# First tiles centred by a broadcast column of sums, first products by halves, the last block by rows

## The chip, the cores and the metric

The kernel runs on one core of a Trainium2 chip. The metric is the device time of one execution in microseconds (us). Engines are named as in the profile: PE is TensorE (matmuls), PEld its weight loads, DVE is VectorE, ACT is ScalarE, POOL is GpSimd, SP is SyncE; SPq, ACTq and POOLq are the places where these issue DMAs. "L694" is line 694 of the kernel before.

## What is computed

Linear attention with a norm, then a two-layer block with layer norm and a residual. There are 8 batches, 8 heads, 576 tokens and 64 features per head, so x has 512 features; the hidden layer has 2048.

```python
kv  = einsum('bhsd,bhse->bhde', k, v)              # 64 x 64 per head
o   = einsum('bhsd,bhde->bhse', q, kv)
x   = o / sqrt(mean(o*o, -1) + 1e-6) * g_norm      # then heads side by side: 512 features
xn  = (x - mean(x)) / sqrt(var(x) + 1e-6) * g_ln
out = x + relu(xn @ w1) @ w2
```

Inputs and output are float32; products run in bf16 and accumulate in float32. The factor 1/sqrt(var) isn't applied to xn: relu lets it pass, so it is multiplied in at the end (`rstd`).

## The kernel before

**Tiles and blocks.** A tile is 128 tokens. Each batch gives four tiles (512 tokens), which are one block; the 64 tokens that are left over in each of the 8 batches form a ninth block, "rem". A tile's path is: `o` (four PE products with kv), `sq` (ACT square), `red` (DVE sum per head), `root` (ACT), reciprocal, `y` and `x` (DVE, scaling), centring (`xc`), and the turn of the centred tile to features by tokens (`xT_blk`), by PE or by DMA. Block b's `mm1(b, ...)` (L684) multiplies `xT_blk` with w1 in groups of one PSUM bank: 16 matmuls with 128 tokens each (one tile at a time, L694), or 4 with 512. ACT applies relu behind each group (L697) and writes m1. `mm2` multiplies m1 with w2.

**mm2 in seven products.** For blocks 1 to 7 and rem, m1 and w2 are seen as 2 x 2 blocks and multiplied with seven products instead of eight (`mm2_seven`, L547, and for rem `mm2_seven_last`, L621). Sums of blocks of m1 (S1 to S4, L515 to L518) come from DVE, sums of blocks of w2 (T1 to T4) were made once. A product is eight matmuls for each of two tiles (`product`, L521, matmuls at L527). p_x and p_y are each made of two products that add up in one bank; of p_y, DVE reads the first product's result (L566) before the second is added.

**Order.** The order of each engine's queue is the order of the program text, written out by hand. `at(slot, fn)` (L769) files a piece of work under a slot of an agenda, and `tick()` (L778), which is called ahead of each group of matmuls, runs what is due. A slot is 1/32 of a block's time; the second half of a block with seven products has 14 ticks, so there slots are pressed together by 14/16. `plan_tile(s, ...)` (L455) files a tile's first part (`o`, `sq`, `red`) at s, its second (reciprocal, `y`, `x`, `xc_w`) at s + 2, and its turn. With at_o = 115 the fourth tile of batch 4 has its first part in tick 110 and its second in tick 112. These lie in batch 3's `mm2`: tick 110 stands ahead of p_q's first tile, 111 ahead of its second; 112 and 113 ahead of p_y's (S2 with T2). S4 (L517) and S3 (L518) are filed at 110 and 111, ahead of anything else in that tick. `var` of another tile (L419, ACT) stands at tick 113, slot 118.1.

**The start.** While the inputs land, the first two tiles of batch 0 go a short way (`x_b`, L318): one DVE instruction makes xb = og / rms in bf16 and sums its rows into `st`. `mean_b` (L326) makes a 128 x 128 diagonal matrix of these sums, for tile 0 on ACT (L330), for tile 1 on DVE (L332). `turn_b` (L334) turns xb by four PE products with the identity and adds to each a product of `mean_sb` (all -1/512, stationary) with that diagonal (moving), which subtracts the mean (L344). Features 0 to 255 are in one bank, 256 to 511 in another. ACT scales the first half with g_ln in two instructions (L355), DVE the second half in one (L357); g_ln by feature, `g_lnT_sb`, comes from a small PE product `glT` (L852) and a DVE copy (L858). `turn_first` and `turn_groups` (L209, L198) turn q of batch 0 by 64 x 64 PE transposes, 16 for each tile. `fill` (L214) puts idle products on PE.

In tick 1, between the first group of `mm1` for tile 0 and that for tile 1, stands `before_1` (L866): the transposes of q for tiles 2 and 3, then `t[1].turn_b()`, then `t[2].o()` and what follows on it. Groups of `mm1` use pool `ps1` with three banks; `t[1].o_g` holds one of them until `t[1].x_g` in tick 2.

**The end.** `mm2_seven_last` (L621) goes through rem's two tiles of each row half one after the other (`for t in range(2)`): for t the products p_x (first), p_q, p_y (first), p_z, p_y (second), store of the second row half (`put(1)`), p_x (second), S4 with b22, store of the first row half (`put(0)`). A `put` issues two DMAs of 64 partitions, one from SP, one from `upper`, ACT or SP. The last S4 product is made in two halves of 128 columns, and the last store in two of 256.

## Time and profile before

| what | value |
|---|---|
| median of 3 runs | 278.20 us (278.18 to 278.21) |
| the profiled execution | 278.19 us |
| its span, first to last instruction | 276.0 us |
| granted PE clock, mean | 0.998 |
| busy PE, DVE, ACT, POOL | 268.8, 197.7, 185.5, 116.6 us |
| first product of `mm1` (L694) | at 14.75 us |
| `mm1` of block 0 to the first product of `mm2` (L716) | 14.75 to 32.43 us |
| `mm2` of batch 3 | 121.7 to 135.8 us |
| `mm2` of rem, its last product | 259.4 to 271.8 us |
| last DVE add | ends at 272.17 us |

The span runs from the first to the last instruction of the program; some 2.2 us of the execution lie outside it. The timeline gives, for each instruction or run of like ones: start, length, engine, line, operation, output<-inputs, shapes, count and, in brackets, how long the engine stood idle before and which event ended that. Matmuls are pipelined: one of 128 columns is recorded with 0.22 us, while they start every 0.056 us. So the length of a run of them is their number times the pace and a drain. The chain is followed back from the last instruction, at each step to what released it.

### The profile page before, as it was taken

The numbers are of one execution on the slowest core, as the hardware profiler recorded it, in microseconds if no ns is written. First come the engines' busy times: TensorE is split into PE (matmuls) and PEld (weight loads), VectorE is DVE, ScalarE is ACT, GpSimd is POOL, SyncE is SP. The second block draws the span as 40 slices with busy tenths as digits, with TensorE's granted clock in tenths as the row PEclk, the third lists the DMA queues.
The fourth block names the chain that finished last, engine by engine and source line by source line (L and its number), as shares of the span: only waits on it lengthen the run. The fifth ranks groups of instructions, "written<-read, shape, count | busy, mean of one in ns | idle before, by whom it ended". The sixth has DMA issues, their size and how long they took to land.

```text
span 276.0 us, 6784 instructions
## 1 busy us (share of the span) xinstructions
PE 268.8 (97%) x2674; PEld 194.8 (71%) x2674; DVE 197.7 (72%) x464; ACT 185.5 (67%) x414; POOL 116.6 (42%) x143
## 2 busy tenths in 40 slices
PE   8899999999999999999999999999999999999993
PEld 3589855999889986468745874587458745874683
DVE  6676437897996895999679856985797379823564
ACT  3567755898759685768576857786877487746610
POOL 8842440991099007901870196017101800280140
PEclk9999999999999999999999999999999999999999
DMA  7999999979979993996299829960711161005032
GB/s 215 199 207 205 197 194 192 202 179 194 113 123 158 184 187 83 151 221 125 31 190 252 116 34 189 246 118 19 171 21 20 21 171 21 20 19 154 1 76 78
DMA packets 63880, 36.57 MB, mean 132 GB/s; under 512 B 34016, under 2 KB 60900, under 8 KB 63848
## 3 DMA queue, kind: packets, MB, share of 16 engines
q0 software_dynamic: 29104, 19.34, 47.9%
q1 hardware_dynamic: 34152, 15.81, 27.8%
q10 hardware_dynamic: 592, 0.98, 1.0%
q8 instruction: 21, 0.34, 0.5%
q14 instruction: 11, 0.09, 0.1%
HBM read 36.71 MB, written 9.44 MB: 167 GB/s over the span
## 4 chain that ended last, share of the span: by engine, by line
PE 84%; DVE 7%; DMA 4%; ACT 2%; issue 1%; POOL 1%; DVEq 0%; POOLq 0%
PE p L694 41%; PE p_y L527 8%; PE p_z L527 8%; PE p_x L527 8%; PE p L716 5%; PE p_s L527 4%; DMA w_sb<-in_moe_w_ch_dram 4%; PE p_q L527 4%; PE o_ps L302 2%; PE kv_ps L275 2%; DVE ss L379 1%; DVE S L517 1%; ACT m L697 1%; DVE o_ps L383 1%; DVE x_blk L401 1%
## 5 line engine op out<-in xcount | busy, mean ns | idle before, releaser
L694 PE MATMUL p<-xT_blk,w_sb 128*128 128x128 bf16 (+2 forms) x1024 | 131.7, 286 | 0.6 <-DMA w_sb<-in_moe_w_ch_dram 0.3
L694 PEld LDWEIGHTS <-w_sb 128*128 128x128 bf16 x1024 | 78.7, 98 | 44.9 <-issue 0.7
L697 ACT ACTIVATE m<-p 128x512 bf16<-128x512 f32 x144 | 85.5, 598 | 35.2 <-PE p L694 33.0
L527 PEld LDWEIGHTS <-m 128*128 128x128 bf16 x512 | 49.4, 98 | 7.7 <-issue 0.6
L379 DVE TENSOR_REDUCE ss<-sq 128x8 f32<-128x512 f32 x35 | 23.8, 680 | 24.6 <-ACT sq L308 24.4
L527 PEld LDWEIGHTS <-S 128*128 128x128 bf16 x392 | 37.5, 98 | 4.5 <-DVE S L516 0.3
L582 POOL TENSOR_TENSOR q<-q,x_blk 128x512 f32<-128x512 f32 x5 | 6.4, 1290 | 69.7 <-ACT q L561 69.7
L527 PE MATMUL p_x<-w_sb,m 128*128 128x256 bf16 x224 | 27.3, 273 | 0.0
L419 ACT ACTIVATE dev<-x_blk,st_blk 128x512 f32<-128x512 f32 x36 | 26.0, 722 | 0.3 <-DVE st_blk L405 0.2
L609 POOL TENSOR_TENSOR u<-u,x_blk 128x512 f32<-128x512 f32 x7 | 8.9, 1268 | 39.5 <-DVE u L566 39.5
L383 DVE TENSOR_TENSOR o_ps<-o_ps,inv 128x512 f32<-128x512 f32 x33 | 23.1, 700 | 3.1
L401 DVE SCALAR_TENSOR_TENSOR x_blk<-o_ps,g_norm_sb 128x512 f32<-128x512 f32 x33 | 22.8, 691 | 1.1
L308 ACT ACTIVATE sq<-o_ps 128x512 f32<-128x512 f32 x35 | 21.0, 599 | 3.6 <-PE o_ps L302 3.6
L515 DVE TENSOR_TENSOR S<-m 128x768 bf16<-128x768 bf16 (+2 forms) x22 | 12.7, 582 | 12.2 <-ACT m L697 12.2
L426 DVE TENSOR_SCALAR xc<-x_blk,st_blk 128x512 bf16<-128x512 f32 x32 | 18.6, 581 | 1.1
L387 ACT ACTIVATE rms<-ss,eps_sb 128x8 f32<-128x8 f32 x36 | 10.8, 299 | 11.7 <-DVE ss L379 11.3
L566 DVE SCALAR_TENSOR_TENSOR u<-p_y,rstd,v 128x256 f32<-128x256 f32 x28 | 12.2, 476 | 5.3 <-PE p_y L527 5.3
L716 PE MATMUL p<-w_sb,m 128*128 128x512 bf16 x64 | 15.0, 379 | 0.0
L561 ACT ACTIVATE v<-p_x,rstd 128x256 f32<-128x256 f32 x28 | 11.0, 478 | 5.3 <-PE p_x L527 5.3
L527 PE MATMUL p_y<-T,m 128*128 128x256 bf16 x112 | 13.9, 272 | 0.2 <-DVE u L566 0.2
L527 PE MATMUL p_z<-w_sb,S 128*128 128x256 bf16 x112 | 13.5, 273 | 0.0
L527 PE MATMUL p_y<-T,S 128*128 128x256 bf16 x112 | 13.5, 273 | 0.0
(149 smaller groups left out, 367.6 us busy)
## 6 DMA issues: line engine op xcount, KB each, us to landing
out_dram<-o_sb SPq DMA_DIRECT2D x26, 256.0 KB, 4.5
w_sb<-in_moe_w_ch_dram POOLq DMA_DIRECT2D x6, 512.0 KB, 13.7
q_in<-in_q_dram POOLq DMA_DIRECT2D x7, 320.0 KB, 6.5
k_in<-in_k_dram POOLq DMA_DIRECT2D x7, 320.0 KB, 7.7
v_in<-in_v_dram POOLq DMA_DIRECT2D x7, 320.0 KB, 9.9
q_in<-in_q_dram POOLq DMA_DIRECT2D x8, 256.0 KB, 7.2
k_in<-in_k_dram POOLq DMA_DIRECT2D x7, 256.0 KB, 8.4
v_in<-in_v_dram POOLq DMA_DIRECT2D x7, 256.0 KB, 12.3
```

What stands on the lines that cost most here:

```text
L308: nc.scalar.activation(self.sq_t, self.o_ps, func=AF.Square)
L379: nc.vector.tensor_reduce(self.ss, self.sq_t, axis=AX.X, op=ALU.add)
L383: nc.vector.tensor_mul(self.o_ps, self.o_ps, self.inv().to_broadcast([128, H, D]))
L401: nc.vector.scalar_tensor_tensor(x_blk[:, ts].rearrange("p (h d) -> p h d", h=H), in0=self.o_ps, scalar=1.0, in1=g_norm_sb.to_broadcast([1 ...
L419: nc.scalar.activation(dev, x_blk[:, ts], func=AF.Square, bias=st[:, 1, ts:ts + 1], accum_out=st[:, 2, ts:ts + 1])
L426: nc.vector.tensor_scalar_add(self.xc_t, x_blk[:, self.ts], st[:, 1, self.ts:self.ts + 1])
L515: for i, fn in enumerate((lambda: nc.vector.tensor_add(S1, a21, a22), lambda: nc.vector.tensor_sub(S2, S1, a11), lambda: nc.vector.tensor_ ...
L527: nc.tensor.matmul(dst[:, t - ts[0], :c1 - c0], lhsT=a[:, i, t * 128:(t + 1) * 128], rhs=w[:, i, c0:c1], start=start and t == ts[0] and i ...
L566: V.scalar_tensor_tensor(dst[:, t], in0=src[:, t], scalar=rstd[:, 2 * rows + t:2 * rows + t + 1], in1=other[:, t], op0=ALU.mult, op1=ALU.add)
L694: nc.tensor.matmul(p1[:, i, :], lhsT=w1_sb[:, kk, de * 128:(de + 1) * 128], rhs=blk[2][:, kk, sl], start=(kk == 0), stop=(kk == nK - 1))
L697: nc.scalar.activation(m1[:, de0:de0 + per, sl], p1, func=AF.Relu)
L716: nc.tensor.matmul(p2[:, c0:c1], lhsT=m1s[b][:, de, ts * 128:(ts + 1) * 128], rhs=w2_sb[:, de, c0:c1], start=(de == 0), stop=(de == nDe - 1))
```

## The change

Six edits:

- `mean_b` makes no diagonal: it copies the tile's sums (one column, 128 x 1) into bf16 `total_sb` on DVE. The centring product has this column, broadcast to 128 columns with step 0, as its stationary operand and `mean_sb` as the moving one; `mean_sb` is now the identity times -1/512, made on DVE behind `four_sb`, and no longer set by a memset at the start.
- `glT` and its copy move up, ahead of `turn_first(1)`.
- `t[0].turn_b()` is written ahead of `t[1].root()`, and in `before_1` `t[1].turn_b()` stands between the transposes for tile 2 and those for tile 3.
- `mm1`: the first group of tiles 0 and 1 goes through features 0 to 255 of all four hidden blocks, then 256 to 511. In all groups only the first matmul has the start flag and only the last the stop flag.
- `mm2_seven_last` becomes a generator with two parts for each tile, taken in the order first part of tile 0, of tile 1, second part of tile 0, of tile 1. Tile 0's `put(1)` now issues both DMAs from SP, and its `put(0)` the upper one from ACT. PSUM banks are taken accordingly.
- The fourth tile of batch 4 is filed at 116.2 instead of 115: first part in tick 111, second in 113, behind the `var` of slot 118.1.

```diff
@@ -129,10 +129,10 @@
     fill_sb = consts.tile([128, 512], bf16)
     gate = consts.tile([1, 1], bf16)
     mean_sb = consts.tile([128, 128], bf16)
+    total_sb = consts.tile([128, 2], bf16)
     gl_rows = consts.tile([nK, 128], f32)
     four_sb = consts.tile([nK, nK], f32)
     g_lnT_sb = consts.tile([128, nK], f32)
-    nc.vector.memset(mean_sb, -1.0 / Dm)
     nc.vector.memset(fill_sb, 0.0)
     nc.sync.dma_start(k_f[:, :HP // 2], pairs(k, 0, HP // 2))
     nc.scalar.dma_start(k_f[:, HP // 2:], pairs(k, HP // 2, HP))
@@ -323,13 +323,10 @@
                 self.xb, in0=self.og_ps, scalar=1.0, in1=self.i, op0=ALU.mult, op1=ALU.mult,
                 accum_out=st[:, 0, self.ts:self.ts + 1])
 
-        def mean_b(self, on_act=False):
-            self.diag = work.tile([128, 128], bf16, tag="diag", name="diag")
-            total = self.blk[1][:, 0, self.ts:self.ts + 1]
-            if on_act:
-                nc.scalar.activation(self.diag, identity, func=AF.Copy, scale=total)
-            else:
-                nc.vector.tensor_scalar_mul(self.diag, identity, total)
+        def mean_b(self):
+
+            ts = self.ts
+            nc.vector.tensor_copy(total_sb[:, ts:ts + 1], self.blk[1][:, 0, ts:ts + 1])
 
         def turn_b(self):
             ts = self.ts
@@ -341,7 +338,7 @@
                                  rhs=identity, start=True, stop=False)
 
             def centred(kk):
-                nc.tensor.matmul(tps[kk // 2][:, kk % 2], lhsT=mean_sb, rhs=self.diag,
+                nc.tensor.matmul(tps[kk // 2][:, kk % 2], lhsT=total_sb[:, ts:ts + 1].to_broadcast([128, 128]), rhs=mean_sb,
                                  start=False, stop=True)
 
             turned(0)
@@ -357,7 +354,7 @@
             nc.vector.tensor_mul(dst[:, 2:], tps[1],
                                  g_lnT_sb[:, 2:].rearrange("p (k o) -> p k o", o=1)
                                  .to_broadcast([128, 2, 128]))
-            del self.xb, self.diag
+            del self.xb
 
 
         def x_g(self, mean=False):
@@ -625,32 +622,34 @@
         b11, b21, b22 = w2_q(0, 0), w2_q(1, 0), w2_q(1, 1)
         x_all, _, o_sb = outs(b)
         v0_t, v1_t, qv_t, w22_t, u2_t = (half(fpool, n, n) for n in ("v0", "v1", "u3", "r5", "u2"))
-        banks = (((ps1, "p1"), (ps1, "p1"), (ps2, "p2"), (ps2, "p2"), (ps_m, "misc")),
-                 ((ps1, "p1"), (ps1, "p1"), (ps_out, "ops"), (ps_out, "ops"), (ps1, "p1"),
-                  (ps2, "p2")))
-        for t in range(2):
+        banks = (((ps1, "p1"), (ps1, "p1"), (ps2, "p2"), (ps2, "p2")),
+                 ((ps1, "p1"), (ps_out, "ops"), (ps_out, "ops"), (ps2, "p2")))
+        ends = (((ps_m, "misc", 0, C2),),
+                ((ps1, "p1", 0, C2 // 2), (ps2, "p2", C2 // 2, C2)))
+
+        def scaled_add(dst, src, r, other):
+            V.scalar_tensor_tensor(dst, in0=src, scalar=r, in1=other, op0=ALU.mult, op1=ALU.add)
+
+        def tile_of(t):
+
             def x(rows, cols):
                 return x_all(rows, cols)[:, t]
 
             def o(rows, cols):
                 return o_sb[rows][:, t, cols * C2:cols * C2 + C2]
 
+            def bank(pool, tag):
+                return pool.tile([128, 1, C2], f32, tag=tag, name="p_s")
+
             def part(dst, a, w, start, stop, c0=0, c1=C2):
                 product(dst, a, w, start, stop, (t,), c0, c1)
 
             def put(rows, c0=0, c1=Dm, upper=nc.scalar):
                 store(b, 2 * rows + t, o_sb[rows][:, t:t + 1], c0, c1, upper)
 
-            ends = ((0, C2),) if t == 0 else ((0, C2 // 2), (C2 // 2, C2))
-            p_x, p_q, p_y, p_z, *p_l = (pool.tile([128, 1, C2], f32, tag=tag, name="p_s")
-                                        for pool, tag in banks[t])
+            p_x, p_q, p_y, p_z = (bank(*e) for e in banks[t])
             v0, v1, qv, w22, u2 = (a[:, t] for a in (v0_t, v1_t, qv_t, w22_t, u2_t))
             r0, r1 = (rstds[b][:, 2 * rows + t:2 * rows + t + 1] for rows in range(2))
-
-            def scaled_add(dst, src, r, other):
-                V.scalar_tensor_tensor(dst, in0=src, scalar=r, in1=other,
-                                       op0=ALU.mult, op1=ALU.add)
-
             part(p_x, a11, b11, True, False)
             nc.scalar.activation(v1, p_x[:, 0], func=AF.Copy, scale=r1)
             nc.scalar.activation(v0, p_x[:, 0], func=AF.Copy, scale=r0)
@@ -667,19 +666,28 @@
             part(p_y, S3, T3, False, True)
             scaled_add(o(1, 0), p_y[:, 0], r1, qv)
             scaled_add(o(1, 1), p_y[:, 0], r1, w22)
-            put(1)
+            put(1, upper=nc.scalar if t else nc.sync)
+            del p_q, p_y, p_z
+            yield
             part(p_x, a12, b21, False, True)
             scaled_add(o(0, 0), p_x[:, 0], r0, x(0, 0))
             if t:
                 put(0, 0, C2)
-            for p, (c0, c1) in zip(p_l, ends):
+            for pool, tag, c0, c1 in ends[t]:
+                p = bank(pool, tag)
                 part(p, S4, b22, True, True, c0, c1)
                 scaled_add(o(0, 1)[:, c0:c1], p[:, 0, :c1 - c0], r0, u2[:, c0:c1])
+                del p
+            del p_x
             if t:
                 put(0, C2)
             else:
-                put(0, upper=nc.sync)
-            del p, p_l, p_x, p_q, p_y, p_z
+                put(0)
+            yield
+
+        tiles = [tile_of(0), tile_of(1)]
+        for t in (0, 1, 0, 1):
+            next(tiles[t])
 
     def mm1(b, t0, n, c0=0, c1=nDe):
         blk, m1 = blks[b], m1_of(b)
@@ -688,12 +696,16 @@
         for de0 in range(c0, c1, per):
             tick()
             p1 = ps1.tile([128, per, n * 128], f32, tag="p1", name="p1")
-            for i in range(per):
+
+            order = ([(i, kk) for k0 in (0, 2) for i in range(per) for kk in (k0, k0 + 1)]
+                     if b == 0 and t0 < 2 and de0 == 0 else
+                     [(i, kk) for i in range(per) for kk in range(nK)])
+            for i, kk in order:
                 de = de0 + i
-                for kk in range(nK):
-                    nc.tensor.matmul(p1[:, i, :], lhsT=w1_sb[:, kk, de * 128:(de + 1) * 128],
-                                     rhs=blk[2][:, kk, sl],
-                                     start=(kk == 0), stop=(kk == nK - 1))
+
+                nc.tensor.matmul(p1[:, i, :], lhsT=w1_sb[:, kk, de * 128:(de + 1) * 128],
+                                 rhs=blk[2][:, kk, sl], start=(i, kk) == order[0],
+                                 stop=(i, kk) == order[-1], skip_group_check=True)
             nc.scalar.activation(m1[:, de0:de0 + per, sl], p1, func=AF.Relu)
             del p1
             if b in (1, 2) and t0 + n == 4 and de0 + per in SPLIT_2:
@@ -788,6 +800,7 @@
     nc.vector.stream_shuffle(g_ln_sb, gl_row, [0] * 32)
     del gl_row
     nc.vector.tensor_copy(four_sb, identity[:nK, :nK])
+    nc.vector.tensor_scalar_mul(mean_sb, identity, -1.0 / Dm)
 
     qts[0] = qt_pool.tile([128, JJ, HP, 128], bf16, tag="qt", name="qt")
     held[0] = kv_pack[0]
@@ -839,6 +852,10 @@
     kv_b.times_g()
     part_red(kv_a)
     part_red(kv_b)
+    glT = ps1.tile([128, nK], f32, tag="p1", name="glT")
+    nc.tensor.matmul(glT, lhsT=gl_rows, rhs=four_sb, start=True, stop=True)
+    nc.vector.tensor_copy(g_lnT_sb, glT)
+    del glT
     turn_first(1, ps_m, "misc")
     t[0].root()
     t[0].o_g(ps2, "p2")
@@ -848,26 +865,22 @@
     turn_first(J, ps_m, "misc")
     t[1].o_g(ps1, "p1")
     fill(1, dead)
-    glT = ps1.tile([128, nK], f32, tag="p1", name="glT")
-    nc.tensor.matmul(glT, lhsT=gl_rows, rhs=four_sb, start=True, stop=True)
     fill(1, dead)
     del dead
     t[0].x_b()
-    t[0].mean_b(True)
+    t[0].mean_b()
     t[1].red()
-    nc.vector.tensor_copy(g_lnT_sb, glT)
-    del glT
+    t[0].turn_b()
     t[1].root()
-    t[0].turn_b()
     t[1].x_b()
     t[1].mean_b()
 
 
     def before_1():
         turn_first(2, ps_m, "misc", nc.vector.tensor_copy)
+        t[1].turn_b()
         tp = ps2.tile([128, HP, 128], bf16, tag="p2", name="tp")
         turn_groups(tp, 3, 0, H)
-        t[1].turn_b()
         t[2].o()
         t[2].sq()
         nc.scalar.copy(qts[0][:, 3], tp)
@@ -962,7 +975,7 @@
     at(268, lambda: rstd_of("rem"))
 
 
-    for b, at_q, at_o in ((3, 52, (68.5, 72.5, 76.5, 83)), (4, 81, (96.5, 102.7, 109, 115)),
+    for b, at_q, at_o in ((3, 52, (68.5, 72.5, 76.5, 83)), (4, 81, (96.5, 102.7, 109, 116.2)),
                           *((b, 32 * b - (46.4 if b == 5 else 47.2), tuple(32 * b - i for i in (34.5, 27.3, 20.1, 12.9)))
                             for b in range(5, B))):
         at(at_q, lambda b=b: turn_q_dma(b))
```

## The prediction

> **What bounds the kernel.** I read the page first (busy time, chain by engine, groups), then the chain in order of time, then the timeline of each engine where the change puts its hand.
>
> ```profile
> PE 268.8 (97%) x2674; PEld 194.8 (71%) x2674; DVE 197.7 (72%) x464; ACT 185.5 (67%) x414; POOL 116.6 (42%) x143
> PE 84%; DVE 7%; DMA 4%; ACT 2%; issue 1%; POOL 1%; DVEq 0%; POOLq 0%
> ...
> L694 PEld LDWEIGHTS <-w_sb 128*128 128x128 bf16 x1024 | 78.7, 98 | 44.9 <-issue 0.7
> ```
>
> TensorE is busy for 97% of the span, so an edit can win only where TensorE waits, or ahead of its first and behind its last product. The change removes no product. It touches three places: the first two tiles (about 13 to 20 us), the second half of batch 3 (121 to 136) and the last block (from 259). A busy share hides stalls there, because a matmul's recorded duration overlaps the next one's; so I measure groups of 16 products by their length.
>
> The profiled execution took 278.19 us, the median is 278.20; 2.2 us lie outside the span and stay.
>
> **First tiles.** Timeline rows of PE, ACT, DVE and POOL, then one row of the chain for the steady pace:
>
> ```profile
> 14.75 1.20 PE L694 MATMUL p<-xT_blk,w_sb 128*128 128x128 bf16 x16 [0.35 <-DMA w_sb<-in_moe_w_ch_dram]
> 15.73 0.22 PE L694 MATMUL p<-xT_blk,w_sb 128*128 128x128 bf16 x1
> 15.88 0.31 PE L204 MATMUL tp<-identity,q_in 64*64 64x64 bf16 x8
> 16.50 0.29 PE L340 MATMUL tp<-identity,xb 128*128 128x128 bf16 x2
> 17.41 1.26 PE L694 MATMUL p<-xT_blk,w_sb 128*128 128x128 bf16 x16
> 18.73 1.06 PE L694 MATMUL p<-xT_blk,w_sb 128*128 128x128 bf16 x16
> 13.14 0.29 PEld L852 LDWEIGHTS glT<-four_sb,gl_rows 4*128 4x128 f32 x2 [0.26 <-issue]
> ...
> 13.45 0.40 ACT L330 ACTIVATE diag<-identity,st_blk 128x128 bf16<-128x128 bf16 x1
> 14.27 0.63 ACT L355 ACTIVATE xT_blk<-tp,g_lnT_sb 128x128 bf16<-128x128 f32 x2
> 16.99 0.63 ACT L355 ACTIVATE xT_blk<-tp,g_lnT_sb 128x128 bf16<-128x128 f32 x2 [0.36 <-PE tp L344]
> 17.51 0.60 ACT L308 ACTIVATE sq<-o_ps 128x512 f32<-128x512 f32 x1
> 18.87 0.30 ACT L387 ACTIVATE rms<-ss,eps_sb 128x8 f32<-128x8 f32 x1 [0.29 <-DVE ss L379]
> 19.08 0.58 ACT L697 ACTIVATE m<-p 128x512 bf16<-128x512 f32 x1
> ...
> 9.31 0.35 DVE L259 CAST kv_pack<-even 64x192 bf16<-64x192 f32 x1 [0.96 <-PE odd L254]
> 13.87 0.15 DVE L858 COPY g_lnT_sb<-glT 128x4 f32<-128x4 f32 x1
> 15.01 0.69 DVE L322 SCALAR_TENSOR_TENSOR xb<-og_ps,inv 128x512 bf16<-128x512 f32 x1
> 15.74 0.54 DVE L332 TENSOR_SCALAR diag<-identity,st_blk 128x128 bf16<-128x128 bf16 x1
> 18.16 0.68 DVE L379 TENSOR_REDUCE ss<-sq 128x8 f32<-128x512 f32 x1
> ...
> 14.98 0.69 POOL L98 DMA_DIRECT2D q_in<-in_q_dram  x1 [1.66 <-DMA w_sb<-in_moe_w_ch_dram]
> 20.67 0.68 POOL L97 DMA_DIRECT2D v_in<-in_v_dram  x1 [1.87 <-DMA w_sb<-in_moe_w_ch_dram]
> ...
> 48.63 0.89 PE p L694 x16
> ```
>
> An undisturbed group takes 1.06 with its drain (18.73). The first two take 1.20 and 1.26: 0.14 and 0.20 lost inside them, waiting for the second half of the turned x.
>
> Tile 0: the 0.40 ACT diagonal goes, and a one-column DVE copy comes (0.15, from L858, the nearest small copy). It starts as soon as x's sum is read out, so the centring products no longer wait for the diagonal that ends at 13.85, and both halves of x are ready about 0.2 earlier. The first product itself doesn't move: it waits for w_sb's landing. Gain: the 0.14 inside the group. By halves, the wait for features 256 to 511 is covered by eight products of 0.056. The glT products (0.29 of loads, some 0.3 in all) only change places with the fill products ahead of the same turn: nothing. They now stand ahead of turn_first(1) and delay its ACT copy and tile 0's root by some 0.05, absorbed because TensorE, not xb, sets that turn. The new mean_sb multiply falls into a DVE wait of 0.96 for the kv products (at most L332's 0.54): nothing.
>
> Tile 1: its root now stands behind tile 0's two L355, so it comes at about 14.57, 0.6 later. DVE's reciprocal stood behind tile 0's multiply until 14.78 anyway; xb ends near 15.83 instead of 15.70, and the column copy at 16.02 instead of the diagonal at 16.28. With half of the 32 small transposes behind it, the turn starts near 16.10 instead of 16.50, L355 at 16.58 instead of 16.99, and the second group ends near 18.29 instead of 18.67: 0.36 to 0.38 ahead at this point.
>
> Most of that is not kept. Behind the turn stands t[2].o(), which now comes no earlier: TensorE goes from full to quarter tiles and back once more (15.73 to 15.88 where the pace is 0.056: 0.10 per switch). Its square (17.51) moves to about 17.42 only, because ACT was its releaser before and the products are now. The chain square, reduction (18.16), root (18.87), then L697 of the second group (19.08, ends 19.66) moves with it by 0.09. The fourth group needs the second's accumulators: the pool has three, and one holds tile 1's og until its x is written. TensorE would reach the fourth group at 18.73 + 0.89 = 19.62, ahead of 19.66; so this end decides already now. **Kept: 0.09.** Above: the third piece of w_sb (POOL's wait for it ends at 20.67; for the first piece POOL resumed at 14.98, 0.23 behind TensorE) lets the fifth group start at about 20.43, 0.15 ahead of the 20.6 that the groups' pace gives now. Below: a broadcast stationary operand has no row. The nearest are LDWEIGHTS of 98 ns and glT's two of 0.15 each; at the latter, four extra loads of 0.05 plus two switches of 0.10 give up to 0.2 lost, through sq of tile 2. I take 98 ns, the same type and width. Range: -0.15 to +0.2.
>
> By the Trainium skill (TensorEngine Tiling (Array Packing), Key Properties) a change of tiling mode drains TensorE. It speaks against turning the second tile between the two groups of small transposes; the rows agree with 0.10 each, and without these drains the 0.09 would be near 0.28.
>
> **Batch 3's second half.** The slot 115 to 116.2 moves the first part of tile (4,3) from the step of p_q's first half to that of its second, and its second part from the first to the second step of p_y. DVE, POOL, ACT and PE rows:
>
> ```profile
> 126.84 0.42 DVE L517 TENSOR_TENSOR S<-m,S 128x512 bf16<-128x512 bf16 x1
> 127.17 0.68 DVE L379 TENSOR_REDUCE ss<-sq 128x8 f32<-128x512 f32 x1
> 127.77 1.07 DVE L518 TENSOR_TENSOR m<-m 128x512 bf16<-128x512 bf16 x1
> 128.77 0.19 DVE L394 RECIPROCAL inv<-rms 128x8 f32<-128x8 f32 x1
> 155.36 0.41 DVE L518 TENSOR_TENSOR m<-m 128x512 bf16<-128x512 bf16 x1
> ...
> 127.29 1.27 POOL L582 TENSOR_TENSOR q<-q,x_blk 128x512 f32<-128x512 f32 x1 [9.43 <-ACT q L561]
> 155.59 1.31 POOL L582 TENSOR_TENSOR q<-q,x_blk 128x512 f32<-128x512 f32 x1 [12.45 <-ACT q L561]
> ...
> 127.89 0.30 ACT L387 ACTIVATE rms<-ss,eps_sb 128x8 f32<-128x8 f32 x1 [0.74 <-DVE ss L379]
> ...
> 130.81 1.05 PE L527 MATMUL p_x<-w_sb,m 128*128 128x256 bf16 x8
> 132.04 1.03 PE L527 MATMUL p_y<-T,m 128*128 128x256 bf16 x8 [0.18 <-DVE u L566]
> ```
>
> Eight products at twice the 0.056 of half the columns end their issue near 131.70; p_y starts at 132.04, so TensorE loses 0.35 here to a late DVE, whose L566 reads p_y's bank first. DVE's order becomes L517, L518, L379 instead of L517, L379, L518. L518 would start at 127.17, 0.12 ahead of POOL's L582, and then cost 0.41, as at 155.36, where it also leads; behind L582 it cost 1.07. The reduction follows at 127.51 to 128.19, the root (no longer covered by L518) at 128.22 to 128.52, the reciprocal at 128.55: 0.21 ahead of 128.77, and so the rest of the tile's second part, L566 and p_y. ACT's order changes only in that L419 goes ahead of the root, into idle time. **Gain 0.21**; the whole wait, 0.35, is the bound.
>
> By the Trainium skill (SBUF — State Buffer, Who interferes with whom) a two-input VectorE instruction and a reading GpSimd one exclude each other, and issue order decides who blocks. The pair of rows at 127 and 155 agrees on the order; a full block would have ended L518 at 128.97, the row ends at 128.84.
>
> **The last block.** By rows instead of by tiles, the same 120 products: the last products and DVE adds keep their order and place. DVE, queue and landing rows:
>
> ```profile
> 271.37 0.80 DVE L651 SCALAR_TENSOR_TENSOR o_sb<-p_s,rstd,u 128x128 f32<-128x128 f32 x2
> 272.19 0.54 SPq L737 DMA_DIRECT2D out_dram<-o_sb  x1
> 271.58 0.79 ACTq L737 DMA_DIRECT2D out_dram<-o_sb  x1
> 272.47 0.56 ACTq L737 DMA_DIRECT2D out_dram<-o_sb  x1
> ...
> out_dram<-o_sb SPq DMA_DIRECT2D x4, 128.0 KB, 2.3
> out_dram<-o_sb ACTq DMA_DIRECT2D x2, 128.0 KB, 2.6
> ```
>
> What moves is the stores: tile 1's second row leaves five steps of eight products after tile 0's, near 269.2, and tile 0's first near 270.6, where ACT's queue now has three stores in a row to the end. So ACT's queue is free when the last add is done, and its last store is issued at 272.2 instead of 272.47: up to 0.27. But a store issued beside SP's lands after 2.6 instead of 2.3, which can take all of it back. No added wait: tile 0's second row goes twice to SP, so tile 1's ACT scaling is not queued behind a store. I take **0.10**; range +0.1 to -0.25.
>
> **Sum:** 278.19 - 0.09 - 0.21 - 0.10 = 277.79, so **277.8**.
>
> **Rivals.**
> A, slower: L518 loses its 0.12 lead over L582. Then it costs 1.07 again, and the root behind the reduction, covered until now, is bare on DVE's path: L518 to 128.25, reduction to 128.85, root to 129.19, reciprocal 129.22, 0.45 later than now. 278.19 - 0.09 + 0.45 - 0.10 = 278.45. For it: a lead of 0.12 in a DVE run that has been without idle time for many us; against it: ACT's q, which releases L582, keeps its place. Chance 0.20; with the first tiles at +0.2 and the stores at +0.1 it reaches 278.9.
> B, more: all three at their upper bounds, 278.19 - 0.15 - 0.35 - 0.25 = 277.44. Against it: each bound needs a second wait to be absent. Chance 0.15.
> C, the change does locally what it says, and nothing arrives: the relu chain holds the fourth group, L518 and L582 meet halfway, the stores land as late as before: 278.15. Chance 0.20.
> Forecast, 277.6 to 278.0: 0.45.
>
> A measurement of this kernel tells about 0.2%, 0.56 us, from no change. Below 277.63: B and the edge of the forecast, 0.20. Above 278.75: the end of A, 0.05. Within: 0.75. Range 277.4 to 278.5; the likeliest case's own is 277.6 to 278.0.
>
> **What would show it.** Right: the first group at 14.75 with 1.06, the second ending near 18.3, but the relu of the second group ending near 19.57; L518 of batch 3 at 0.41 and ahead of POOL; the wait ahead of p_y near 0.14; ACT's last store at 272.2 less the shift. Wrong: a first product that starts away from w_sb's landing; LDWEIGHTS of total_sb above 98 ns; L518 at 1.07; a landing of the last store that keeps its distance to the end.

## The result and the profile after

| | before | after |
|---|---|---|
| median, run by turns on one chip | 278.49 us (11 runs) | 277.72 us (11 runs) |
| ratio after / before, 95% interval | | 0.9976 [0.9968, 0.9984] |
| the profiled execution | 278.19 us | 277.72 us |
| its span | 276.0 us | 275.5 us |

The forecast was 277.8 within 277.4 to 278.5. As a difference it was 0.4 us; the ratio says 0.67 us (0.45 to 0.89), since the kernel before took a little longer in these runs than in the three shown at first. The changed kernel is faster by about as much as this measurement can tell.

The page of the changed kernel, its first part and its chain:

```profile
PE 267.1 (97%) x2658; PEld 194.8 (71%) x2674; DVE 197.3 (72%) x465; ACT 184.9 (67%) x413; POOL 116.0 (42%) x143
...
PE 92%; DMA 3%; ACT 2%; DVE 1%; issue 1%; POOLq 0%
```

The busy shares are those of before; sixteen matmuls are merely missing in the record. The chain has changed: DVE's share falls from 7% to 1% and PE's rises from 84% to 92%. That is the stretch up to p_y in batch 3: the chain used to leave TensorE there for a long run of DVE work, and now it doesn't.

**First tiles**, timeline of the changed kernel (start, length, engine, line, operation, count, idle time before and its end; mm1's products are now L706, ACT's scalings L352, DVE's L354, relu L709):

```profile
10.21 0.19 PE L254 MATMUL odd<-v_in,k_in 64*64 64x64 bf16 x1
14.63 1.25 PE L706 MATMUL p<-xT_blk,w_sb 128*128 128x128 bf16 x16 [0.29 <-ACT xT_blk L352]
18.46 1.06 PE L706 MATMUL p<-xT_blk,w_sb 128*128 128x128 bf16 x16
19.73 1.05 PE L706 MATMUL p<-xT_blk,w_sb 128*128 128x128 bf16 x16 [0.21 <-ACT m L709]
...
14.21 0.63 ACT L352 ACTIVATE xT_blk<-tp,g_lnT_sb 128x128 bf16<-128x128 f32 x2 [0.42 <-PE tp L341]
...
14.37 0.42 DVE L354 TENSOR_TENSOR xT_blk<-tp,g_lnT_sb 128x256 bf16<-128x256 f32 x1
...
17.54 0.60 ACT L308 ACTIVATE sq<-o_ps 128x512 f32<-128x512 f32 x1 [0.24 <-PE o_ps L302]
20.82 0.60 ACT L709 ACTIVATE m<-p 128x512 bf16<-128x512 f32 x1 [0.65 <-PE p L706]
...
16.25 0.10 PEld L341 LDWEIGHTS <-total_sb 128*128 128x128 bf16 x1
```

The third group starts 0.27 sooner (18.46 against 18.73), and at the pace of 0.056 the fourth could follow at 18.46 + 0.89 = 19.35. It stands at 19.73, 0.38 late, where the kernel before has 19.71. At first sight the start brought nothing. But the two executions didn't begin alike: the last product of k and v, which waits for v to land, comes at 10.21 here and at 10.06 in the kernel before:

```profile
10.06 0.19 PE L254 MATMUL odd<-v_in,k_in 64*64 64x64 bf16 x1
...
20.80 0.60 ACT L697 ACTIVATE m<-p 128x512 bf16<-128x512 f32 x1 [0.38 <-PE p L694]
```

Everything at the start hangs on that landing, so I count from the last kv product. A good mark is the relu of the fourth group: 20.80 - 10.06 = 10.74 before, 20.82 - 10.21 = 10.61 after. The start is 0.13 shorter, and the later landing of v hid it in this pair of traces. Six of the seven profiles with the old start have 10.73 to 10.75 at this mark. The seventh, e1 below, has 10.66; there the last kv product itself came late, 0.88 behind DVE's first cast of kv, where all the other profiles have 0.74.

**Batch 3**, the same kernel (S3 is now L515, POOL's add L579, the reduction L376):

```profile
127.20 0.42 DVE L515 TENSOR_TENSOR m<-m 128x512 bf16<-128x512 bf16 x1
127.53 0.68 DVE L376 TENSOR_REDUCE ss<-sq 128x8 f32<-128x512 f32 x1
128.57 0.20 DVE L391 RECIPROCAL inv<-rms 128x8 f32<-128x8 f32 x1 [0.37 <-ACT rms L384]
...
127.31 1.43 POOL L579 TENSOR_TENSOR q<-q,x_blk 128x512 f32<-128x512 f32 x1 [10.09 <-ACT q L558]
...
130.84 1.05 PE L524 MATMUL p_x<-w_sb,m 128*128 128x256 bf16 x8
131.86 1.03 PE L524 MATMUL p_y<-T,m 128*128 128x256 bf16 x8
```

S3 starts 0.11 ahead of POOL's add, takes 0.42, and the reciprocal comes 0.20 sooner. p_x to p_y is 1.02 where it was 1.23. From here on every product of TensorE is 0.18 ahead of before.

**The end**: last add, then the last store of each queue alone, then its landing (KB, us from issue to landing):

```profile
271.64 0.35 DVE L631 SCALAR_TENSOR_TENSOR o_sb<-p_s,rstd,u 128x128 f32<-128x128 f32 x1
...
272.02 0.62 ACTq L749 DMA_DIRECT2D out_dram<-o_sb  x1
...
272.02 0.47 SPq L749 DMA_DIRECT2D out_dram<-o_sb  x1
```

```profile
out_dram<-o_sb ACTq DMA_DIRECT2D x1, 64.0 KB, 2.2
```

Both queues issue 0.03 behind the end of the last add (271.99). Before, ACT's stood 0.30 behind it (272.47 against 272.17). From the end of the last add to the end of the span it is 275.52 - 271.99 = 3.53, and was 276.04 - 272.17 = 3.88: the end is 0.35 shorter.

The sum of the three: 0.13 + 0.20 + 0.35 = 0.68, the ratio's 0.67, whose interval of 0.45 to 0.89 is too wide to check the sum so closely. The two profiled executions differ by 0.47 only, because v landed 0.15 later in the second.

### The profile page after: what moved, and what is told of

It reads as the page before. It is cut to its first block, busy times and chain, and to the rows that moved or that the text cites. A ratio compares the mean times of both kernels' runs of the same rounds, so it can differ in the third digit from the quotient of the medians.

```text
span 275.5 us, 6766 instructions
## 1 busy us (share of the span) xinstructions
PE 267.1 (97%) x2658; PEld 194.8 (71%) x2674; DVE 197.3 (72%) x465; ACT 184.9 (67%) x413; POOL 116.0 (42%) x143
## 4 chain that ended last, share of the span: by engine, by line
PE 92%; DMA 3%; ACT 2%; DVE 1%; issue 1%; POOLq 0%
PE p L706 44%; PE p_x L524 9%; PE p_y L524 9%; PE p_z L524 9%; PE p L728 5%; PE p_s L524 4%; PE p_q L524 4%; PE o_ps L302 3%; DMA v_in<-in_v_dram 3%; PE kv_ps L275 2%; ACT m L709 1%; PE tp L204 1%; DVE ss L376 1%; ACT sq L308 0%; PE tp L430 0%
## 5 line engine op out<-in xcount | busy, mean ns | idle before, releaser
L706 PE MATMUL p<-xT_blk,w_sb 128*128 128x128 bf16 (+2 forms) x1012 | 131.0, 285 | 1.3 <-ACT xT_blk L352 0.3
L706 PEld LDWEIGHTS <-w_sb 128*128 128x128 bf16 x1024 | 78.7, 98 | 44.8 <-issue 1.3
L709 ACT ACTIVATE m<-p 128x512 bf16<-128x512 f32 x144 | 85.4, 598 | 35.0 <-PE p L706 33.0
L376 DVE TENSOR_REDUCE ss<-sq 128x8 f32<-128x512 f32 x35 | 23.8, 680 | 25.0 <-ACT sq L308 24.8
L579 POOL TENSOR_TENSOR q<-q,x_blk 128x512 f32<-128x512 f32 x5 | 6.6, 1324 | 70.4 <-ACT q L558 70.4
```

Source lines behind the costliest of these rows:

```text
L376: nc.vector.tensor_reduce(self.ss, self.sq_t, axis=AX.X, op=ALU.add)
L706: nc.tensor.matmul(p1[:, i, :], lhsT=w1_sb[:, kk, de * 128:(de + 1) * 128], rhs=blk[2][:, kk, sl], start=(i, kk) == order[0], stop=(i, kk) ...
L709: nc.scalar.activation(m1[:, de0:de0 + per, sl], p1, func=AF.Relu)
```

## The experiments

### Each part alone

**e1_slot**: the kernel before with one edit.

```diff
-(4, 81, (96.5, 102.7, 109, 115))
+(4, 81, (96.5, 102.7, 109, 116.2))
```

> The kernel before with only the slot of tile (4,3) moved from 115 to 116.2. Theory (port and order): in batch 3 the S3 subtraction (L518) runs ahead of POOL's q add (L582) and takes 0.41 instead of 1.07, and the wait ahead of p_y falls from 0.35 to about 0.15; all of the 0.20 that the changed kernel shows there comes from this edit, so the span is 0.20 below the kernel before (ratio about 0.9993). Rival (the start or another part shifts the lead of L518 over L582): alone, the edit leaves L518 near 1.07, the root behind the reduction is bare, and the time is up to 0.4 longer.

Measured: 278.05 us, ratio 0.9993 [0.9985, 1.0002]. DVE and PE rows:

```profile
127.19 0.42 DVE L518 TENSOR_TENSOR m<-m 128x512 bf16<-128x512 bf16 x1
...
130.83 1.05 PE L527 MATMUL p_x<-w_sb,m 128*128 128x256 bf16 x8
131.86 1.03 PE L527 MATMUL p_y<-T,m 128*128 128x256 bf16 x8
```

0.42 and a wait of 0.15, the same as with all edits together. The rival falls: its price doesn't show.

**e2_end**: the kernel before with the new `mm2_seven_last` alone (its diff stands above).

> The kernel before with only the last block in the new order. Theory (ACT's queue): ACT's last store is issued at about 272.2 instead of 272.47 and lands at least 0.3 earlier; the span falls by 0.33 to 0.38 (ratio about 0.9987). Rival (the end gained nothing by itself, landings only vary from run to run by some 0.3): the last landing keeps its distance of 2.57 to the last add (272.17 to 274.74), span within 0.1 of the kernel before.

Measured: 277.98 us, ratio 0.9986 [0.9974, 0.9998]. ACT's last store in its timeline:

```profile
272.33 0.62 ACTq L748 DMA_DIRECT2D out_dram<-o_sb  x1
```

It stands 0.03 behind the add (272.30) again, with 3.54 to the end of the span. The end gains 0.33 by itself, the largest of the three parts.

**e3_start**: the changed kernel with the old `mm2_seven_last` and the old slot.

```diff
-(4, 81, (96.5, 102.7, 109, 116.2))
+(4, 81, (96.5, 102.7, 109, 115))
```

> The changed kernel with the slot back at 115 and the last block in the old order, so the edits of the first tiles alone. Theory (relu behind tile 2's root): second and third group 0.07 and 0.27 earlier, the fourth waits 0.38 for the second group's relu and stands at 19.73, within 0.03 of the kernel before; nothing arrives, time the same within 0.05 us beside the run's own spread. Rival (the straggling piece of w_sb in the profile of before, 14.70, was typical and the changed start gains by itself): time 0.1 to 0.2 below the kernel before.

Measured: 278.29 us, ratio 0.9995 [0.9987, 1.0004]. Its timeline, last kv product and relu of the fourth group:

```profile
10.38 0.19 PE L254 MATMUL odd<-v_in,k_in 64*64 64x64 bf16 x1
...
21.00 0.60 ACT L698 ACTIVATE m<-p 128x512 bf16<-128x512 f32 x1 [0.66 <-PE p L695]
```

10.62, as in the changed kernel (10.61). My theory was half wrong: the fourth group does wait 0.38 for the relu, but the start is shorter by 0.13 all the same; by the clock it starts at 19.91, 0.2 later than before, because v landed later still. The three ratios add up to 0.9974, the whole has 0.9976. Only e2's interval lies clear of 1, so the size of each part rests on the traces.

### What the start's 0.13 is made of

**e11_column**: two of the start's edits undone.

```diff
-order = ([(i, kk) for k0 in (0, 2) for i in range(per) for kk in (k0, k0 + 1)]
-         if b == 0 and t0 < 2 and de0 == 0 else
-         [(i, kk) for i in range(per) for kk in range(nK)])
+order = [(i, kk) for i in range(per) for kk in range(nK)]
...
-        t[1].turn_b()
         tp = ps2.tile([128, HP, 128], bf16, tag="p2", name="tp")
         turn_groups(tp, 3, 0, H)
+        t[1].turn_b()
```

> The changed kernel with two edits of the first tiles undone: the first groups' products in the old order (not by halves of x), and t[1].turn_b() back behind the transposes for tile 3. Of the start there remain the broadcast column in place of the diagonal, the earlier glT and tile 0's turn ahead of tile 1's root. Theory (the column gives the whole gain; the halves give nothing, since the second product already waits for ACT's second scaling, of features 128 to 255): second product of the first group waits 0.2 as in the changed kernel, and the fourth group stands 9.54 behind the last kv product, where the kernel before has 9.65 and the changed kernel 9.53. Rival (the halves cover DVE's half of x and give the gain): fourth group at 9.60 or later.

Measured (a single run): 277.91 us. Its timeline, last kv product, first group, relu of the fourth:

```profile
10.15 0.19 PE L254 MATMUL odd<-v_in,k_in 64*64 64x64 bf16 x1
14.57 1.25 PE L704 MATMUL p<-xT_blk,w_sb 128*128 128x128 bf16 x16 [0.29 <-ACT xT_blk L352]
...
20.68 0.60 ACT L707 ACTIVATE m<-p 128x512 bf16<-128x512 f32 x1 [0.38 <-PE p L704]
```

20.68 - 10.15 = 10.53: sooner than with both edits (10.61), which neither side of the expectation had. So what is left of the start (the column, the earlier glT and tile 0's earlier turn, which no run takes apart) gives 0.21, more than the whole, and the two edits undone here cost 0.08. The first group is 1.25 long with halves and without.

**e12_halves_small**: the halves back, the turn still behind the transposes, slot at 115; and in the old last block a test of the end.

```diff
-        t[1].turn_b()
         tp = ps2.tile([128, HP, 128], bf16, tag="p2", name="tp")
         turn_groups(tp, 3, 0, H)
+        t[1].turn_b()
...
-            put(1)
+            put(1, 0 if t == 0 else 384)
```

> Two questions at two ends that don't touch each other: the start of the changed kernel with only t[1].turn_b() put back (the first products stay by halves), slot at 115, and the last block in the old order with tile 1's store of its second row cut to its last 128 columns (three quarters of these 128 rows of the output are left out), so that it is issued as late as in the kernel before. Start, theory (the halves give nothing, moving the turn up costs 0.09): fourth group 9.43 behind the last kv product, as with the halves undone too, against 9.53 in the changed kernel; rival (the halves cost or gain): 9.5 or more, or 9.38 or less. If the first piece of w_sb lands late (first product 4.6 behind the last kv product instead of 4.42) this one is not told. End, theory (queue): ACT's last store comes 0.30 behind the last add as in the kernel before and the stretch from the last add to the end of the span is 3.8 to 3.9; rival (bytes in flight): issues as before, stretch near 3.55.

Measured (a single run): 278.06 us. The same rows of its timeline:

```profile
10.07 0.19 PE L254 MATMUL odd<-v_in,k_in 64*64 64x64 bf16 x1
14.68 1.07 PE L695 MATMUL p<-xT_blk,w_sb 128*128 128x128 bf16 x16 [0.48 <-DMA w_sb<-in_moe_w_ch_dram]
...
20.60 0.60 ACT L698 ACTIVATE m<-p 128x512 bf16<-128x512 f32 x1 [0.38 <-PE p L695]
```

10.53 again. So **the halves give nothing, and moving tile 1's turn up costs 0.08**. Here w_sb did land late (first product 4.61 behind the last kv product, else 4.42), the case that I had set aside; it costs nothing, because the group then runs without its inner wait (1.07 instead of 1.25) and ends at the same time. The second group has its inner wait by halves too: it is 1.25 long here, and 1.26 in e11 without them.

**e7_turn_back**: the changed kernel with only this put back.

```diff
-        t[1].turn_b()
         tp = ps2.tile([128, HP, 128], bf16, tag="p2", name="tp")
         turn_groups(tp, 3, 0, H)
+        t[1].turn_b()
```

> The changed kernel with t[1].turn_b() put back behind the transposes for tile 3, so two switches of tile size less in the first tiles. Theory (relu chain decides): the second group starts as in the kernel before, about 0.05 later than in the changed kernel, tile 2's square starts behind ACT's L352 as before, and the fourth group stands within 0.06 of the changed kernel, counted from the last kv product: no difference in time. Rival (the two more drains of 0.10 cost what the earlier turn gains; without them the start gains more): fourth group 0.15 or more earlier, time 0.15 to 0.2 below the changed kernel.

Measured: 277.65 us, ratio 0.9975 [0.9964, 0.9985], the changed kernel's. 20.74 - 10.11 = 10.63, which looks like my theory. But by the list of waits this profile has one that e11 and e12 lack:

```profile
PEld L204 <- DMA q_in<-in_q_dram: 0.2, 1, 0.2
```

The small transposes waited for q's second half to land. That puts them 5.71 behind the last kv product, in e12 5.61; with these 0.10 taken off it would be 10.53 once more. The 0.10 is carried on unchanged: tile 2's products stand 6.79 behind the last kv product against 6.69 in e11 and e12, the third group 8.56 against 8.46. By this reckoning, which no run without that landing repeats, e7 agrees with e11 and e12; its theory, that the drains cost nothing, rests on a start held up by that landing.

**e4_o_first**: the changed kernel with tile 2's products ahead of the second set of small transposes.

```diff
         t[1].turn_b()
+        t[2].o()
+        t[2].sq()
         tp = ps2.tile([128, HP, 128], bf16, tag="p2", name="tp")
         turn_groups(tp, 3, 0, H)
-        t[2].o()
-        t[2].sq()
```

> The changed kernel with t[2].o() and its square ahead of the second set of 64 x 64 transposes (turn_groups(3)) instead of behind it; the number of switches of tile size stays. Theory (the gain of the first tiles is given back in the chain o, square, reduction, root, relu of the second group): tile 2's products start at about 16.75 instead of 17.11, its square at about 17.33 (behind ACT's L352) instead of 17.54, the root at about 18.68 and the fourth group at 19.50 to 19.55 instead of 19.73; all later products come 0.17 to 0.2 earlier, bounded by the third piece of w_sb (landing at 20.40, fifth group not ahead of 20.43), so about 0.2 us less than the changed kernel, 0.6 to 0.7 less than the kernel before. Rival (the four switches of tile size and the drains hold it, not the relu): the fourth group stays within 0.05 of 19.73, and the time is that of the changed kernel.

Measured: 277.64 us, ratio 0.9973 [0.9965, 0.9982]. Its timeline, last kv product, ACT, and the weight loads of the fifth group:

```profile
10.05 0.19 PE L254 MATMUL odd<-v_in,k_in 64*64 64x64 bf16 x1
...
17.13 0.60 ACT L308 ACTIVATE sq<-o_ps 128x512 f32<-128x512 f32 x1
...
20.51 0.60 ACT L709 ACTIVATE m<-p 128x512 bf16<-128x512 f32 x1 [0.30 <-PE p L706]
21.59 0.60 ACT L709 ACTIVATE m<-p 128x512 bf16<-128x512 f32 x1 [0.48 <-PE p L706]
...
20.48 0.90 PEld L706 LDWEIGHTS <-w_sb 128*128 128x128 bf16 x16 [0.18 <-DMA w_sb<-in_moe_w_ch_dram]
```

The chain o, square, root, relu is what held the fourth group: with the square at 7.08 behind the last kv product instead of 7.33 the fourth group's relu comes at 10.46 instead of 10.61, and the fourth group waits for nothing. The fifth group's relu then follows 1.08 later, where the pace is 0.89: 0.19 given back at once. TensorE's own row shows no wait there, but that of its weight loads does: 0.18 for w_sb to land. In e8 below, which has the same start 0.3 later by the clock, the fifth follows after 0.91. This profile has e7's wait for q too (small transposes at 5.67 instead of 5.61). The expected 0.2 doesn't arrive: the time isn't told apart from the changed kernel's.

### What the batch's 0.20 is made of

**e5_q_late**: the kernel before, slot at 115, in batch 3 alone POOL's add of q behind that of u2.

```diff
             scaled(q, p_q, 1)
-            add(q, q, x(1, 0))
+            if b == 3:
+                late.append(lambda: G.tensor_add(q, q, x(1, 0)))
+            else:
+                add(q, q, x(1, 0))
```

> The kernel before, slot still 115; in batch 3 alone POOL's add q + x (L582) is issued behind the add of u2 instead of in front of it, so that no POOL add runs beside L518. Theory (DVE's subtraction L518 and POOL's add exclude each other, whoever comes first keeps the port): L518 takes 0.41 from 127.77 behind the reduction, the reciprocal comes at about 128.2 instead of 128.77, and the wait ahead of p_y (0.35) goes wholly, since 0.57 is gained on DVE and only 0.35 is needed; span 0.35 below the kernel before, more than the 0.20 of the slot. Rival (L518's 1.07 has another cause, such as the reduction or the root beside it): L518 stays near 1.07 and the wait ahead of p_y at 0.35.

Measured: 278.07 us, ratio 0.9989 [0.9979, 0.9998]. Timeline rows; the first two, of the start, are used further below:

```profile
10.49 0.19 PE L254 MATMUL odd<-v_in,k_in 64*64 64x64 bf16 x1
15.12 1.26 PE L697 MATMUL p<-xT_blk,w_sb 128*128 128x128 bf16 x16 [0.29 <-ACT xT_blk L355]
...
127.63 0.68 DVE L379 TENSOR_REDUCE ss<-sq 128x8 f32<-128x512 f32 x1
128.23 0.41 DVE L518 TENSOR_TENSOR m<-m 128x512 bf16<-128x512 bf16 x1
...
131.27 1.05 PE L527 MATMUL p_x<-w_sb,m 128*128 128x256 bf16 x8
132.15 1.04 PE L527 MATMUL p_y<-T,m 128*128 128x256 bf16 x8
```

L518 stands where it stood, behind the reduction, and takes 0.41 instead of 1.07, with nothing moved but POOL's add. p_x to p_y is 0.88: the wait is gone, 0.35 gained where the slot gains 0.20. The cause of the 1.07 is shown to be POOL's add beside it; reduction and root are cleared.

### What the end's 0.35 is made of

**e10_put_sp**: the kernel before; ACT has two stores at the end and SP four.

```diff
-            put(1)
+            put(1, upper=nc.sync if t else nc.scalar)
```

> The kernel before; both halves of tile 1's store of its second row are issued by SP, so that ACT has two stores near the end and SP four. Bytes and order stay. Theory (a queue that is still issuing sets the end): ACT's last store comes at 272.19, right behind the add, but SP's last one waits for three earlier issues of about 0.55 and comes at 272.6 or later; the stretch from the last add to the end of the span is 4.0 or longer. Rival (bytes in flight): stretch as before, 3.85 to 3.9.

Measured (a single run): 279.07 us, 4.14 from the last add (272.78) to the end. The last store of each queue in its timeline:

```profile
272.81 0.49 ACTq L737 DMA_DIRECT2D out_dram<-o_sb  x1
...
273.56 0.66 SPq L737 DMA_DIRECT2D out_dram<-o_sb  x1
```

ACT's last store now comes in time and SP's 0.78 late; counted from the last add, the span ends 0.27 later than in the kernel before. (The other 0.61 of the longer span arose ahead of the edit: 0.43 is v's later landing, and 0.18 arose near 219 us, where TensorE's weight loads stood idle for 0.27.) With the same bytes in flight, the late issue sets the end.

**e12's end**: the store of tile 1's second row with a quarter of its bytes (the rest of these rows is left out of the output), issued as late as before. ACT's last store in the timeline, then its row in the list of DMA issues:

```profile
272.59 0.56 ACTq L738 DMA_DIRECT2D out_dram<-o_sb  x1
```

```profile
out_dram<-o_sb ACTq DMA_DIRECT2D x1, 64.0 KB, 2.0
```

Issued 0.31 behind the last add (272.28) as before, but landed 2.0 after the issue instead of 2.3; 3.63 to the end. My theory (3.8 to 3.9) falls short: bytes in flight count too, for 0.24. By the Trainium skill (DMA: Bandwidth & Descriptors, Queues, rings and completion order) a store reports only behind every earlier write of its DMA engines; this run agrees with that, and doesn't tell it from an effect of the smaller traffic alone.

**e9_put_small**: the same test made badly, in the kernel before.

```diff
-            put(1)
+            put(1, 0, Dm if t == 0 else 128)
```

> The kernel before; tile 1's store of its second row (two DMAs at 270.99, from SP and ACT) carries 128 of its 512 columns, so three quarters of these 128 rows of the output are left out. The issues stay as many and in their order, the bytes in flight behind them fall by 192 KB. Theory (ACT's queue): ACT's last store still comes at about 272.47 and the stretch from the end of the last add to the end of the span stays at 3.85 to 3.9. Rival (bytes in flight): the stretch falls to about 3.55, as in the new order of the last block, with the issues where they were.

Measured (a single run): 278.03 us, 3.55. It tells nothing apart: the first 128 columns are done one add sooner, so the store was issued 0.39 sooner, ACT's queue was free in time and its last store stood 0.03 behind the add. Both theories give 3.55 then. e12 took the last columns instead.

**e6_put_pool**: the kernel before with one half of that store issued by POOL.

```diff
-            put(1)
+            put(1, upper=nc.gpsimd if t else nc.scalar)
```

> The kernel before; of tile 1's store of its second row (at 270.99) the upper half is issued by POOL instead of ACT. Bytes and order of the stores stay, only ACT's queue has one store less. Theory (ACT's queue): ACT's last store is issued right behind the last add (272.19 instead of 272.47), and the stretch from the end of the last add to the end of the span falls from 3.88 to about 3.55, as in the new order of the last block. Rival (fewer bytes in flight at the end, which the new order gives by storing tile 1's second row 1.9 us earlier): the issue comes earlier, but the landing is as late as before, stretch 3.8 or more.

Measured: 279.33 us, ratio 1.0035 [1.0022, 1.0047]. From its list of DMA issues at the end (KB, us to landing, median):

```profile
out_dram<-o_sb POOLq DMA_DIRECT2D x1, 128.0 KB, 3.1
out_dram<-o_sb ACTq DMA_DIRECT2D x2, 64.0 KB, 3.0
```

ACT's last store did come 0.03 behind the add, but with a store from POOL among them all that come behind it land after 2.7 to 3.3. 4.44 to the end: neither theory, and no use for telling them apart.

So of the end's 0.35, ACT's late issue is 0.27; the rest is a slightly sooner landing. Either part alone (e10's ACT store in time, e12's fewer bytes) is not the whole, and they don't simply add: 0.27 and 0.24 make 0.35 together.

### A version from what was learned

**e8_best**: the changed kernel with e4's and e5's edits (shown there) and the old slot.

```diff
-(4, 81, (96.5, 102.7, 109, 116.2))
+(4, 81, (96.5, 102.7, 109, 115))
```

> A version meant to beat both: the changed kernel with tile 2's products ahead of the second set of small transposes (as in e4), and in batch 3 the slot back at 115 with POOL's q add behind that of u2 (as in e5). Theory: wait ahead of p_y gone (0.15 less than the changed kernel), fourth group without a wait, fifth bounded by the third piece of w_sb at 20.4; 0.15 to 0.3 less than the changed kernel, 277.4 to 277.6. Rival (L518 has another cause, and the piece of w_sb holds the rest): wait ahead of p_y back at 0.35, time 0.1 above the changed kernel.

Measured: 277.57 us, ratio 0.9976 [0.9965, 0.9988]. Its timeline:

```profile
10.37 0.19 PE L254 MATMUL odd<-v_in,k_in 64*64 64x64 bf16 x1
...
20.76 0.60 ACT L712 ACTIVATE m<-p 128x512 bf16<-128x512 f32 x1 [0.30 <-PE p L709]
```

The fourth group's relu is at 10.39 and p_y follows p_x by 0.88 (130.78 to 131.66), both as meant. It beats the kernel before; against the changed kernel the times don't tell it apart (277.57 and 277.72). Why so little of a sooner start arrives is seen in e11, which like e12 was early by the clock (timeline):

```profile
46.76 0.40 PE L302 MATMUL o_ps<-kv_pack,qt 128*128 128x128 bf16 x4 [0.20 <-DMA qt<-q_p]
```

At 46.5, in block 1, TensorE needs batch 2's q as transposed by DMA. That DMA is issued behind a DVE copy, which waits for q to land (timeline of e11):

```profile
31.50 0.83 DVE L918 COPY q_p<-q_in 128x2560 bf16<-128x2560 bf16 x1 [4.55 <-DMA q_in<-in_q_dram]
```

So it has a time of its own, which a sooner start doesn't move: the copy stands between 31.27 and 31.50 in all fourteen profiles. In the kernel before, these products stand at 46.52 and in the changed one at 46.54, without idle time on TensorE; e11 waits until 46.76, e12 until 46.63. The weight loads ahead of these products wait even where the products' own row shows nothing (changed kernel, then e4; in the kernel before it is 0.17):

```profile
46.45 0.30 PEld L302 LDWEIGHTS <-qt 128*128 128x128 bf16 x4 [0.24 <-DMA qt<-q_p]
46.55 0.23 PEld L302 LDWEIGHTS <-qt 128*128 128x128 bf16 x4 [0.47 <-DMA qt<-q_p]
```

e4's products come at 46.55 and e7's, behind a wait of 0.41, at 46.62, though the fourth group's relu was sooner by the clock than in the changed kernel, by 0.31 and 0.08. So in e4, e7, e11 and e12 what the start gained by the clock is given back here. In e8, where the inputs landed later, the loads don't wait.

## Why the prediction was right, and where not

**Batch 3 (0.21 forecast, 0.20 measured): right, step by step.** The order of DVE, the lead of L518 (0.12 forecast, 0.11), its price (0.41 forecast, 0.42), the reciprocal at 128.55 (128.57) and the wait left ahead of p_y (0.14, measured 0.15). Its mechanism, which was read from two rows, was tested alone by e5. The root that lost its cover (0.37 of idle ahead of the reciprocal) was in the sum and is in the trace. Rival A, the lost lead, came in none of the runs with the slot at 116.2.

**First tiles (0.09 forecast, 0.13 measured): the size nearly right, two of its steps wrong.**
- "The first product itself doesn't move: it waits for w_sb's landing." It moves, which the prediction had named as a sign of being wrong, by 0.21 (4.42 behind the last kv product in the changed kernel, 15.12 - 10.49 = 4.63 in e5, which has the old start): it waits for ACT's first scaling. In the one profile of before, w_sb's first piece was late; in ten of the fourteen profiles it was there in time. And a late piece costs nothing, as e12 shows; in the kernel before the mark is 10.74 with a late piece and without one.
- "By halves, the wait for features 256 to 511 is covered." There was none to cover: the second product waits for ACT's second scaling, which writes features 128 to 255 and ends at 14.83, later than DVE's half (14.80). Only the second quarter of x is late, so a cut behind the first half covers nothing.
- "Most of that is not kept", because the second group's relu stands behind tile 2's root: right, and shown by e4.
- The drains. By the Trainium skill (TensorEngine Tiling (Array Packing), Key Properties) a change of tiling mode drains TensorE, and the prediction put the start without them near 0.28; e11 and e12, without the two extra switches, have 0.21 against 0.13. Tile 2's products stand 6.90 behind the last kv product in the changed kernel and 6.69 in e11 and e12, about the two switches of 0.10; of these 0.21 the relu of the fourth group keeps 0.08. So the direction is right: this edit of the change costs 0.08.
- The broadcast column as stationary operand loads in 0.10 like any other: the choice of 98 ns was right.

**The last block (0.10 forecast, 0.35 measured): the step that failed.** "A store issued beside SP's lands after 2.6 instead of 2.3, which can take all of it back." The issue came 0.27 sooner, as worked out, but the discount was read from the wrong store. 2.6 is the median of two stores of 128 KB; ACT's last one, of 64 KB, landed after 2.3 in the kernel before and after 2.2 now. With no discount this term would have been 0.27, and the bytes that are out of the way 1.9 us sooner fit the rest. Its bound of 0.25 was too small as well.

**The total.** 0.40 forecast, 0.67 by the ratio. The absolute time came closer (277.8 and 277.72) than the difference, because the kernel before was slower in the runs side by side than in the three that the forecast began from. That closeness is luck: the base was 0.29 lower than the kernel before in the runs side by side, and the forecast gain 0.27 too small.

## What to carry to other kernels

Count a start from the landing that sets it off, not from the span's first instruction: 0.13 of gain was invisible until then. Where two engines hold each other off, look at who starts first, and move the one that nobody waits for (POOL's add, 0.35) rather than the one on the path (the tile, 0.20). Ahead of the last store, see that each queue is free when the last add ends, and take a landing time from a store in the same place, not from a median.

## What the runs showed of the hardware

- The landing of the first inputs varies: the last kv product stands between 10.05 and 10.49 us in fourteen profiles, with old and new start alike. This alone is more than any part of the change.
- ACT's queue took 0.79 to issue a store of 64 KB that came 0.59 behind the one ahead of it, and 0.51 to 0.54 where the distance was 0.8 or more. In e12, where the store ahead carried only 32 KB, it took 0.79 as well. SP's took 0.55 against 0.47. That is how three stores in a row made ACT's last one late.
- A DVE instruction held off by POOL doesn't wait for the end of POOL's record: L518 ended 0.28 behind it, though alone it takes 0.41. The other way round POOL's add grew from 1.27 to 1.43, by 0.16, though S3 overlaps 0.30 of it. The Trainium skill (SBUF — State Buffer, Who interferes with whom) calls the port pair that the two engines share an exclusive lock. By the records here the block is shorter than the overlap by 0.13 to 0.14 in both cases.
- With one store from POOL among those of SP and ACT at the end (e6), the four stores behind it landed after 2.7 to 3.3, where the last ones of the kernel before took 2.3 to 2.8, and the stretch behind the last add grew by 0.56, from 3.88 to 4.44. The time grew by 1.0 us. In the profiles the span grew by 1.13: beside the 0.56, 0.31 is a later landing of v, and 0.26 arose near 219 us, ahead of the edit, where TensorE's weight loads stood idle for 0.36; no run shows the cause of that.
